# Another order of score stretches, sums and products in two hand-written turns of a two-layer attention and mixer kernel

## The chip, the cores and the metric

The kernel runs on one core of one Trainium2 chip. The metric is the device time of one execution in microseconds (us). Before the change the median of three runs was 2517.36 us, with the lowest at 2516.68 and the highest at 2517.88.

## The reference, cut to what matters

Two layers, each an attention (32 heads of 16 columns, one common key and value) and a token mixer, over 2048 tokens of 512 columns in float32:

```python
def _A_ref(x, wq, wk, wv, wo):          # B, S, D = 1, 2048, 512; H = 32, Dh = 16
    q = (x @ wq).reshape(B, S, H, Dh).transpose(0, 2, 1, 3)
    k, v = x @ wk, x @ wv
    scores = jnp.einsum("bhqd,bkd->bhqk", q, k) * (Dh ** -0.5)
    o = jnp.einsum("bhqk,bkd->bhqd", _softmax(scores, axis=-1), v)
    return o.transpose(0, 2, 1, 3).reshape(B, S, H * Dh) @ wo

def _B_ref(x, w1, b1, w2, b2):          # F = 1792
    u = _gelu(jnp.einsum("bsd,sf->bdf", _layernorm(x), w1) + b1)
    return (jnp.einsum("bdf,fs->bds", u, w2) + b2).transpose(0, 2, 1)

x = x + _A_ref(_layernorm(x), ...); x = x + _B_ref(_layernorm(x), ...)   # twice
```

## The kernel before, in words

**Stretches and groups.** The attention of a layer is cut into 1,024 stretches. A stretch holds the scores of two heads for 128 keys and 512 queries, which is a tile of 128x1024. There are 32 groups (four blocks of 512 queries, eight groups of four heads in each) of 32 stretches (16 key tiles, two pairs of heads). A stretch goes through three engines:

- `scores` (L903): TensorE (PE) makes the scores in a PSUM tile `sc` (matmuls at L909). There are three such tiles (`bank2`, two banks each), so a stretch can only be begun when the stretch three before it has been read out.
- ScalarE (ACT) takes the exponential out of `sc` into a tile `p` in SBUF (L919). In a "copied" stretch VectorE (DVE) first copies `sc` to `p` (L917) and ACT then works in place in `p`; the PSUM tile is free once the copy is done.
- `sums` (L921): PE multiplies `p` by the values into the accumulator `acc` of the group (L925). Two stretches of one key tile lie on different columns of the array. Stretches that are scored and not yet summed stand in `pend`; there are 8 tiles `p`, and 4 more from stretch 256 on.

**Products.** Between the stretches PE does matrix products of six matmuls of 128x128x512 each: the projections of finished heads with `wo` (tile `po`, L886, added to `x` by DVE at L894) and products of the mixer's first layer (tile `pu`, L1202; two of them make one result, which DVE copies or adds into `ua` at L1208 or L1210). DVE also does the normalization of rows of `x` that are finished (statistics at L1115 and L1116, the root at L218 to L233 and L203, the rows `hb` at L239, L1127 and L1131), the division of finished heads (L845 to L851) and the splitting of mixer weights (L1187, L1189). These small jobs wait in the list `steps`; `Mixer.step` takes jobs from it up to a budget.

**Turns.** The order of all this is written out by hand in tuples, called turns. `Attention.run` picks one when the last is done and goes through it: a number k above zero scores k stretches (13 is three, of which the last is copied; 12 is two, of which the last is copied); 0 is a product; -k sums the k oldest stretches of `pend` and then lets DVE do some of `steps`. The instructions of each engine stand in the order in which the turn names them, and each engine goes through its own in that order. In the queue of SyncE (SP) stand the loads of queries (`load_group`, issued when the second stretch of a group has been scored), of weights `w1r` and the moves of finished groups.

**Which turn is taken.** `to_boundary` is the number of stretches that must be summed until the group is finished. `PLAIN` (2, -2) is the turn when there is nothing to mix in. Up to stretch 270 two stretches stand in `pend` between turns (`LAG`); later four (once `normed` is above zero, the first block of rows being partly normalized). At stretch 270 of a layer, with 268 summed (`to_boundary` 20), the four projections of the first block's last heads are ready, and `Mixer.turn` returns `QUAD_TO_FOUR` with four projections: 32 stretches are scored and 30 summed, which takes `pend` from two to four. Four `PLAIN` turns follow, in which the last normalization of the block is done. At stretch 310, with 306 summed (`to_boundary` 14), the first two mixer products come, in the turn `COPIED`, 16 stretches long; a `DOUBLE` (32 stretches and four mixer products) is next. In the trace each of these two places comes once per layer: `QUAD_TO_FOUR` at 314.32 us and 1561.69 us, the first `pu` at 355.18 us and 1602.54 us.

Of the kernel before, what the change touches and what calls it, by code (L numbers as in the profile page):

```python
# [32 lines left out]
KEPT = 6  # L33
# [4 lines left out]
WHOLE = (13, 0, 0, 13, -4, 13, -4, 13, -4)  # L38
LONG = (2, 0, 13, -4, 13, -4, 13, 0, 13, -4, 12, -4)
COPIED = (13, 0, 12, 0, 13, -4, 13, -4, 3, -4, 2, -4)  # L40
DOUBLE = (
    13, -4, 13, 0, 0, 13, -4, 13, -4, 13, -4, 13, 0, 13, -4, 13, -4, 12, 0, 13, -4, 13, -4,
)
QUAD = (13, -4, 13, 0, 3, -6, 13, 0, 13, -4, 3, -4, 12, 0, 13, 0, 13, -6, 13, -4, 13, -4)
QUAD_TO_FOUR = (3, -2) + QUAD[2:]
FOURS = (3, -4, 12, 0, 13, 0, -4, 3, -4, 12, 0, 13, -4, 0)
SHORT = (2, 0, 3, -4, 3, -4)
TINY = (2, 0, 2, -4)
PLAIN = (2, -2)
# [20 lines left out]
def kernel(  # L70
# [18 lines left out]
    def pool(name, bufs=1, side="left"):  # L89
        return tc.alloc_tile_pool(name=name, bufs=bufs, side=side, reuse_waits="tile")  # L90
# [9 lines left out]
    def bank(i, name):  # L100
        return ps.tile([P, QB], F32, tag=f"ac{i % 2}", name=name)
# [146 lines left out]
    class Proj:  # L248
# [113 lines left out]
        def turn(self, ts_):  # L362

            self.transposes(ts_)
            self.first_rows(ts_)
            self.second_rows(ts_)
# [279 lines left out]
        def later(self, att):  # L646
# [3 lines left out]
            def put(turn, parts):  # L650
                work.append((turn, parts, None))
# [139 lines left out]
    class Attention:  # L791
# [185 lines left out]
        def size(self, turn):  # L977
            return sum(k % 10 for k in turn if k > 0)
# [6 lines left out]
        def run(self, mix, proj):  # L985


            total = 2 * NKT * NG * NB
            guards = [2 * NKT * g for g in sorted({2 * FIRST[self.l], NG})] + [total]
            self.guards = guards  # L990
            later, guarded, flagged = proj.later(self), 0, 0

            rest = range(NB - 2 if self.l == 0 else NB - 1, NB)
            turn, queued = FIRST_TURN[self.l], False
            parts = [lambda i, b=b: proj.values(b, i) for b in rest]
            while self.scored < total:
                mix.chores(self)
                ahead = min(t for t in guards if t > self.scored)
                known = ahead < guards[-2] or not later
                if ahead < total and self.scored >= ahead - 16 and flagged < ahead and known:  # L1000
                    flagged = ahead
                    proj.flag(proj.flagged)
                if turn is None:
                    turn = PLAIN
                    self.lag = 2 * LAG if mix.normed and self.scored < total - 16 else LAG
                    if len(self.pend) == self.lag:
                        after, queued = None, bool(later) and not mix.projections
                        if queued:
                            turn, parts, after = later[0]
                            if turn is WHOLE and self.to_boundary() >= 14 and self.slack(later) >= 4:  # L1010
                                turn = LONG
                        else:
                            turn, parts = mix.turn(self)
                            if turn is COPIED and not self.spares:
                                turn = LONG
                    left = min(t - self.scored for t in guards if t > self.scored)
                    if queued and turn is LONG and left < self.size(LONG):
                        turn = WHOLE
                    if left < self.size(turn):
                        turn = PLAIN  # L1020
                        if parts and mix.projections and left >= sum(k for k in SHORT if k > 0):
                            turn, parts = SHORT, parts[:1]
                    if turn in (LONG, COPIED) and self.to_boundary() in (2, 4, 2 * NKT):
                        turn = PLAIN
                    if turn is WHOLE and self.to_boundary() == 2:
                        turn = PLAIN
                parts = list(parts)
                for k in turn:
                    if k > 0:
                        self.more(mix, k)  # L1030
                    elif k == 0:
                        if queued and turn is TINY:
                            mix.step(2.0, self)
                        parts.pop(0)(self.spare())
                        if turn is DOUBLE and len(parts) % 2:
                            mix.step(1.0, self)
                        if queued and not parts:
                            later.pop(0)
                            if after:
                                after()  # L1040
                            if not later:
                                proj.close()
                                mix.open()
                    else:
                        if turn is PLAIN:
                            k = -min(4, max(0, len(self.pend) - self.lag))
                        end = self.to_boundary() <= -k
                        busy = self.behind
                        if busy:
                            self.behind = None  # L1050
                            busy()
                        self.drain(-k)
                        mix.chores(self)
                        if busy and turn is not DOUBLE:
                            continue
                        if self.pieces:
                            self.pieces.pop(0)()
                        elif turn in (LONG, COPIED, DOUBLE, QUAD, QUAD_TO_FOUR, FOURS, WHOLE):
                            room = 2.4 if turn in (COPIED, QUAD, QUAD_TO_FOUR) else 1.0
                            mix.step(min(room, 0.8 * self.to_boundary()), self)  # L1060
                        elif end:
                            mix.step(2.0, self)
                assert self.scored < guards[-2] or not later
                if self.scored in guards[:-1] and self.scored > guarded:
                    guarded = self.scored
                    i = guards.index(guarded)
                    proj.guard(guarded // (2 * NKT), guards[i + 1] // (2 * NKT))
                    if mix.opened:
                        self.spares = pool(f"more{self.l}")
                if turn is PLAIN and self.to_boundary() > 4:  # L1070
                    mix.step(1.7 if mix.normed else 2.4, self)
                turn = None


    class Mixer:
# [150 lines left out]
        def turn(self, att):  # L1226

            def projection(i):
                self.projection(att, i)

            def first(i):
                self.pu = bank(i, f"pu{self.l}_{self.done}")
                self.product(self.pu, stop=False)
                self.following()

            def second(_):
                r, f = self.product(self.pu, start=False)
                self.add(self.pu, r - 1, f)
                att.behind = self.following

            early = att.spares and att.scored < 2 * NKT * (NB * NG - 2) + 8
            if early and len(self.projections) > 3 and len(att.pend) == LAG and att.to_boundary() == 20:
                return QUAD_TO_FOUR, [projection] * 4
            early = early and att.to_boundary() in (26, 28, 30)
            if early and len(self.projections) > 3:
                return QUAD, [projection] * 4
            if len(self.projections) > 3 and att.to_boundary() == 30 and att.scored > 2 * NKT * (NB * NG - 1):
                return FOURS, [projection] * 4
            if len(self.projections) > 1:
                return COPIED, [projection] * 2  # L1250
            if self.projections:
                return SHORT, [projection]
            if early and (self.ready(KEPT + 1, 2) or self.last_pair_behind()):
                return DOUBLE, [first, second] * 2
            even = not att.spares or att.to_boundary() in (14, 30)
            return (COPIED, [first, second]) if even and self.ready(KEPT) else (PLAIN, [])

        def projection(self, att, which):

# [205 lines left out]
        def after(self, s):  # L1465
            self.split2(2 * s + 4)
# [115 lines left out]
    for layer in range(2):  # L1582
# [63 lines left out]
        if more:  # L1646
# [17 lines left out]
            second = proj.queries(b - 1, 1)  # L1664
# [59 lines left out]
```

## Time and profile before

| | |
|---|---|
| median of three runs | 2517.36 us |
| the profiled execution | 2514.03 us |
| its span, first to last instruction | 2512.3 us |
| PE busy | 2492.7 us (99%) |
| ACT busy | 2102.8 us (84%) |
| DVE busy | 1550.9 us (62%) |
| exponentials out of PSUM (L919, `p<-sc`) | 1444 of 1048 ns |
| exponentials of copied stretches (L919, `p<-p`) | 604 of 1084 ns |
| copies (L917) | 604 of 1224 ns |
| granted TensorE clock, mean | 0.999 |

How to read it: the span is one execution as the hardware profiler saw it, and the 1.73 us between it and the execution's own time lie before its first and after its last instruction. A busy PE is not a PE at its peak: its matmuls are pipelined, their ends are modelled, and a matmul that waits inside a run can be counted as busy. What a run of matmuls costs is therefore read below from the start of one run to the start of the next. In the timeline a line is start, duration, engine, source line, operation, tiles, shapes and the number of instructions merged; a bracket at its end tells how long the engine stood idle before it and who ended that. PE's count per stretch is two matmuls for scores and four for sums.

### The profile page before, as it was taken

The numbers are of one execution on the slowest core, as the hardware profiler recorded it, in microseconds if no ns is written. First come the engines' busy times: TensorE is split into PE (matmuls) and PEld (weight loads), VectorE is DVE, ScalarE is ACT, GpSimd is POOL, SyncE is SP. The second block draws the span as 40 slices with busy tenths as digits, with TensorE's granted clock in tenths as the row PEclk, the third lists the DMA queues.
The fourth block names the chain that finished last, engine by engine and source line by source line (L and its number), as shares of the span: only waits on it lengthen the run. The fifth ranks groups of instructions, "written<-read, shape, count | busy, mean of one in ns | idle before, by whom it ended". The sixth has DMA issues, their size and how long they took to land. (4 is left out here: it accounts for less than half of the span.)

```text
span 2512.3 us, 41954 instructions
## 1 busy us (share of the span) xinstructions
PE 2492.7 (99%) x16158; PEld 1240.3 (49%) x16158; DVE 1550.9 (62%) x2458; ACT 2102.8 (84%) x2344; POOL 147.8 (6%) x235
## 2 busy tenths in 40 slices
PE   9999999999999999999999999999999999999999
PEld 6444334444444444588863443344444444445887
DVE  6565566667766776564445664666677667765522
ACT  6999999999999999653349999999999999995511
POOL 5000000000000000141000000000000000002200
PEclk9999999999999999999999999999999999999999
DMA  3221201111111111134423211111111111102343
GB/s 116 75 66 41 65 27 41 31 42 31 39 31 39 31 41 31 43 110 149 128 58 118 61 45 48 31 39 31 41 31 39 31 42 33 40 26 66 107 125 95
DMA packets 168679, 143.56 MB, mean 57 GB/s; under 512 B 17650, under 2 KB 132368, under 8 KB 167952
## 3 DMA queue, kind: packets, MB, share of 16 engines
q1 hardware_dynamic: 168464, 140.72, 19.3%
q8 instruction: 132, 2.16, 0.4%
q14 instruction: 83, 0.68, 0.1%
HBM read 97.67 MB, written 26.22 MB: 49 GB/s over the span
## 5 line engine op out<-in xcount | busy, mean ns | idle before, releaser
L919 ACT ACTIVATE p<-sc 128x1024 f32<-128x1024 f32 x1444 | 1404.4, 1048 | 62.6 <-PE sc L909 61.9
L917 DVE COPY p<-sc 128x1024 f32<-128x1024 f32 x604 | 739.1, 1224 | 520.8 <-PE sc L909 436.8
L925 PE MATMUL acc<-p,vaug 128*32 128x512 f32 x8192 | 999.3, 599 | 0.5 <-DVE q L528 0.5
L909 PE MATMUL sc<-qs,kst 51*128 51x512 f32 x4096 | 684.9, 432 | 10.2 <-ACT p L919 3.3
L919 ACT ACTIVATE p<-p 128x1024 f32<-128x1024 f32 x604 | 654.8, 1084 | 16.4 <-DVE p L917 11.0
L909 PEld LDWEIGHTS sc<-qs,kst 51*128 51x128 f32 x4096 | 338.1, 184 | 564.3 <-ACT p L919 393.8
L925 PEld LDWEIGHTS acc<-p,vaug 128*32 128x32 f32 x8192 | 218.8, 109 | 488.7 <-issue 472.5
L1455 PE MATMUL py<-u,w 128*128 128x512 f32 x1344 | 307.4, 390 | 0.0
L1455 PEld LDWEIGHTS py<-u,w 128*128 128x128 f32 x1344 | 251.9, 188 | 52.3
L1443 ACT CAST w<-w2r 128x896 fp32r<-128x896 f32 x64 | 60.3, 945 | 184.9 <-PE py L1455 177.3
L1202 PE MATMUL pu<-hb,w 128*128 128x512 f32 x792 | 209.6, 406 | 0.0
L1202 PEld LDWEIGHTS pu<-hb,w 128*128 128x128 f32 x792 | 140.9, 188 | 57.6 <-issue 31.1
L1189 POOL TENSOR_TENSOR w<-w1r,w 128x256 fp32r<-128x256 f32 x86 | 69.7, 818 | 1586.1 <-ACT w L1187 1584.0
L1444 DVE TENSOR_TENSOR w<-w2r,w 128x896 fp32r<-128x896 f32 x64 | 71.9, 1123 | 111.5 <-ACT w L1443 111.2
L845 DVE RECIPROCAL o<-o 128x128 f32<-128x128 f32 x120 | 113.3, 944 | 8.7 <-DMA o<-ev 8.7
L886 PE MATMUL po<-wo,hl 128*128 128x512 f32 x360 | 100.3, 412 | 0.1
L827 DVE COPY ev<-acc 128x512 f32<-128x512 f32 x64 | 43.7, 683 | 69.1 <-PE acc L925 69.1
L415 PE MATMUL pq<-hT,wq 128*128 128x512 f32 x312 | 81.1, 404 | 0.0
L886 PEld LDWEIGHTS po<-wo,hl 128*128 128x128 f32 x360 | 62.6, 188 | 33.6 <-issue 15.9
L1202 PE MATMUL pu_l<-hb,w 128*128 128x512 f32 x336 | 77.1, 389 | 0.0
L1461 DVE SCALAR_TENSOR_TENSOR x<-py,b2c,x 128x512 f32<-128x512 f32 x32 | 24.0, 750 | 81.2 <-PE py L1455 81.2
L1187 ACT CAST w<-w1r 128x256 fp32r<-128x256 f32 x86 | 34.4, 406 | 47.2 <-PE pu_l L1202 12.8
(191 smaller groups left out, 1179.3 us busy)
## 6 DMA issues: line engine op xcount, KB each, us to landing
w1r<-in_B_w_dram SPq DMA_DIRECT2D x224, 128.0 KB
w2r<-in_B_w_dram SPq DMA_DIRECT2D x64, 448.0 KB
qs<-qd SPq DMA_DIRECT2D x384, 64.0 KB
qd<-q SPq DMA_DIRECT2D x64, 256.0 KB
o<-ev SPq DMA_DIRECT2D x128, 128.0 KB
x<-in_A_x_dram SPq DMA_DIRECT2D x16, 256.0 KB
hd<-hT SPq DMA_DIRECT2D x2, 2048.0 KB
out_dram<-x SPq DMA_DIRECT2D x16, 256.0 KB
```

The lines of the kernel that those rows point to most:

```text
L415: yield nc.tensor.matmul(out, a, c, start=(k == 0), stop=(k == len(terms) - 1))
L845: nc.vector.reciprocal(o[:, 1, c], o[:, 1, c])
L886: nc.tensor.matmul(po, a, c, start=(k == 0), stop=(k == 3 * len(parts) - 1))
L909: nc.tensor.matmul(sc[:, j, :], kst[kt // 4][rows, kt % 4 * P : (kt % 4 + 1) * P], qs[i % NQ][rows, j0 // 2, :], start=True, stop=True,)
L917: nc.vector.tensor_copy(pt, sc)
L919: nc.scalar.activation(pt, sc, AF.Exp, scale=0.25)
L925: nc.tensor.matmul(self.acc[i][c : c + 32, :], vaug[:, kt].rearrange("p d k -> p (d k)"), pt[:, j, :], start=(kt == 0), stop=(kt == NKT - ...
L1189: eng.tensor_tensor(w[:, 1], raw, f32(w[:, 0]), op=ALU.subtract)
L1202: nc.tensor.matmul(pu, a, c, start=(start and k == 0), stop=(stop and k == 5))
L1443: nc.scalar.copy(w[:, 0], raw)
L1444: nc.vector.tensor_tensor(w[:, 1], raw, f32(w[:, 0]), op=ALU.subtract)
L1455: nc.tensor.matmul(py, a, d, start=(c == 0 and f == 0 and k == 0), stop=(c == 1 and f == NFH - 1 and k == 2),)
```

## The change

Two tuples and the places that name them. `QUAD_TO_FOUR` had been `QUAD` with another first pair of entries; it is now written out in an order of its own. `ENTRY` is new and takes the place of `COPIED` where `Mixer.turn` returns a pair of mixer products; projections that use `COPIED` keep it. `ENTRY` is given the same budget for `steps` as `COPIED`.

```diff
 QUAD = (13, -4, 13, 0, 3, -6, 13, 0, 13, -4, 3, -4, 12, 0, 13, 0, 13, -6, 13, -4, 13, -4)
-QUAD_TO_FOUR = (3, -2) + QUAD[2:]
+QUAD_TO_FOUR = (
+    2, -2, 13, 0, 13, -4, 13, 0, 13, -4, 3, -6, 13, 0, 13, 0, 3, -6, 13, -4, 3, -4,
+)
+ENTRY = (1, 0, 13, 0, 13, -4, 13, -4, 13, -4, 13, -4)
...
-                        elif turn in (LONG, COPIED, DOUBLE, QUAD, QUAD_TO_FOUR, FOURS, WHOLE):
-                            room = 2.4 if turn in (COPIED, QUAD, QUAD_TO_FOUR) else 1.0
+                        elif turn in (LONG, COPIED, ENTRY, DOUBLE, QUAD, QUAD_TO_FOUR, FOURS, WHOLE):
+                            room = 2.4 if turn in (COPIED, ENTRY, QUAD, QUAD_TO_FOUR) else 1.0
...
-            return (COPIED, [first, second]) if even and self.ready(KEPT) else (PLAIN, [])
+            return (ENTRY, [first, second]) if even and self.ready(KEPT) else (PLAIN, [])
```

Written one above the other, before and after:

```
stretch 270, before: 3 -2 13 0  3 -6 13 0 13 -4 3 -4 12 0 13 0 13 -6 13 -4 13 -4
stretch 270, after:  2 -2 13 0 13 -4 13 0 13 -4 3 -6 13 0 13 0  3 -6 13 -4  3 -4
stretch 310, before: 13 0 12 0 13 -4 13 -4  3 -4  2 -4
stretch 310, after:   1 0 13 0 13 -4 13 -4 13 -4 13 -4
```

## The prediction

> **What bounds the kernel now.** The page comes first: the span and the share of PE.
>
> ```profile
> span 2512.3 us, 41954 instructions
> ...
> PE 2492.7 (99%) x16158; PEld 1240.3 (49%) x16158; DVE 1550.9 (62%) x2458; ACT 2102.8 (84%) x2344; POOL 147.8 (6%) x235
> ...
> L1202 PE MATMUL pu<-hb,w 128*128 128x512 f32 x792 | 209.6, 406 | 0.0
> ```
>
> PE is counted busy for 99% of the span, but a matmul that waits inside a run is counted too, so the page cannot show whether the two turns lose anything. The table by stretches of time puts a number on it: the two changed turns and the four `PLAIN` turns between them, in layer 0, then a `DOUBLE` cycle for comparison, then the same three in layer 1.
>
> ```profile
> 314.32:345.45 31.13, 30.59 (x211) 12.65 (x210) 20.81 (x42) 29.74 (x32) 0.00 (x0) 1.00 0.07 22
> 345.45:353.42 7.97, 7.23 (x52) 2.11 (x48) 6.88 (x22) 7.27 (x9) 0.00 (x0) 1.00 0.01 3
> 353.42:369.80 16.38, 15.96 (x113) 6.38 (x109) 7.53 (x10) 16.00 (x18) 0.00 (x0) 1.00 0.15 42
> 741.73:772.30 30.57, 30.57 (x218) 12.92 (x216) 24.17 (x38) 29.62 (x33) 0.00 (x0) 1.00 0.14 40
> 1561.69:1592.81 31.12, 30.59 (x212) 12.64 (x210) 20.94 (x42) 29.75 (x32) 0.00 (x0) 1.00 0.08 22
> 1592.81:1600.79 7.98, 7.24 (x53) 2.11 (x49) 6.88 (x22) 7.28 (x9) 0.00 (x0) 1.00 0.01 2
> 1600.79:1617.13 16.34, 15.93 (x112) 6.39 (x108) 7.53 (x10) 15.98 (x18) 0.00 (x0) 1.00 0.15 42
> ```
>
> The first number after the window is its length. The changed region takes 31.13 + 7.97 + 16.38 = 55.48 us in layer 0 and 31.12 + 7.98 + 16.34 = 55.44 in layer 1, so one walk serves both. The clock is 1.00 in all of them. What it would take without a wait comes from PE's timeline, read from the start of one run to the start of the next.
>
> ```profile
> 312.49 0.73 PE L909 MATMUL sc<-qs,kst 51*128 51x512 f32 x4
> 313.15 1.24 PE L925 MATMUL acc<-p,vaug 128*32 128x512 f32 x8
> 314.32 1.35 PE L909 MATMUL sc<-qs,kst 51*128 51x512 f32 x6
> 315.60 1.07 PE L925 MATMUL acc<-p,vaug 128*32 128x512 f32 x8
> 316.60 0.91 PE L909 MATMUL sc<-qs,kst 51*128 51x512 f32 x4
> 317.92 0.49 PE L909 MATMUL sc<-qs,kst 51*128 51x512 f32 x2 [0.42 <-ACT p L919]
> 318.34 1.67 PE L886 MATMUL po<-wo,hl 128*128 128x512 f32 x6
> 319.94 0.97 PE L909 MATMUL sc<-qs,kst 51*128 51x512 f32 x6
> 320.84 2.78 PE L925 MATMUL acc<-p,vaug 128*32 128x512 f32 x24
> 323.55 0.97 PE L909 MATMUL sc<-qs,kst 51*128 51x512 f32 x6
> 324.45 1.65 PE L886 MATMUL po<-wo,hl 128*128 128x512 f32 x6
> 326.03 0.96 PE L909 MATMUL sc<-qs,kst 51*128 51x512 f32 x6
> 326.93 1.92 PE L925 MATMUL acc<-p,vaug 128*32 128x512 f32 x16
> 328.78 0.96 PE L909 MATMUL sc<-qs,kst 51*128 51x512 f32 x6
> ...
> 345.45 0.73 PE L909 MATMUL sc<-qs,kst 51*128 51x512 f32 x4
> 346.11 1.06 PE L925 MATMUL acc<-p,vaug 128*32 128x512 f32 x8
> 347.11 0.49 PE L909 MATMUL sc<-qs,kst 51*128 51x512 f32 x2
> 348.34 0.49 PE L909 MATMUL sc<-qs,kst 51*128 51x512 f32 x2 [0.74 <-ACT p L919]
> 348.77 1.06 PE L925 MATMUL acc<-p,vaug 128*32 128x512 f32 x8
> ...
> 353.42 0.90 PE L909 MATMUL sc<-qs,kst 51*128 51x512 f32 x4
> 354.75 0.50 PE L909 MATMUL sc<-qs,kst 51*128 51x512 f32 x2 [0.42 <-ACT p L919]
> 355.18 1.67 PE L1202 MATMUL pu<-hb,w 128*128 128x512 f32 x6
> ```
>
> Without a wait, three score stretches take 326.93 - 326.03 = 0.90, two 346.11 - 345.45 = 0.66, one 348.77 - 348.34 = 0.43; two sums 347.11 - 346.11 = 1.00, four 328.78 - 326.93 = 1.85, six 323.55 - 320.84 = 2.71; a product 326.03 - 324.45 = 1.58. As a test, `DOUBLE` is ten runs of three, one of two, eight of four sums and four products: 9.00 + 0.66 + 14.80 + 6.32 = 30.78, and its window took 30.57, so it waits for nothing. `QUAD_TO_FOUR` is ten runs of three, one of two, two, four times four and twice six sums, four products: 9.00 + 0.66 + 1.00 + 7.40 + 5.42 + 6.32 = 29.80. Four `PLAIN` are 4 x 1.66 = 6.64. `COPIED` is 3.60 + 1.32 + 7.40 + 3.16 = 15.48. Together that is 51.92 against 55.48: **3.56 us of waiting per layer**, 1.33 in `QUAD_TO_FOUR`, 1.33 in the `PLAIN` turns, 0.90 in `COPIED`.
>
> Where they lie can be read in the same rows. The run of three at 314.32 takes 1.28 and the next one, at 316.60, takes 1.74 until the product at 318.34: 0.38 and 0.84 too long. The `PLAIN` at 347.11 needs 1.66 for its two scores instead of 0.66, and `COPIED`, at 353.42, 1.76 for three instead of 0.90. All of them wait for a PSUM tile that ACT, or the copy on DVE, has not yet emptied. ACT and DVE at these places:
>
> ```profile
> 302.18 17.52 ACT L919 ACTIVATE p<-sc 128x1024 f32<-128x1024 f32 x19 [0.83 <-PE sc L909]
> 319.77 1.06 ACT L919 ACTIVATE p<-p 128x1024 f32<-128x1024 f32 x1
> 320.73 2.83 ACT L919 ACTIVATE p<-sc 128x1024 f32<-128x1024 f32 x3
> ...
> 346.32 1.06 ACT L919 ACTIVATE p<-p 128x1024 f32<-128x1024 f32 x1 [0.70 <-DVE p L917]
> 347.28 9.24 ACT L919 ACTIVATE p<-sc 128x1024 f32<-128x1024 f32 x10
> ...
> 370.40 1.94 ACT L919 ACTIVATE p<-sc 128x1024 f32<-128x1024 f32 x2 [0.35 <-PE sc L909]
> ```
>
> ```profile
> 344.26 0.69 DVE L1115 BATCH_NORM_STATS2 stb<-x 128x6 f32<-128x512 f32 x1
> ...
> 345.08 1.20 DVE L917 COPY p<-sc 128x1024 f32<-128x1024 f32 x1
> ```
>
> ACT runs without a gap from 302.18 through 19 exponentials, 17.52 / 19 = 0.92 each, and a copied one costs 320.73 - 319.77 = 0.96. A `PLAIN` gives ACT 1.84 of work in 1.66 of PE's, so PE is held back to ACT's pace before stretch 270 (312.49 to 314.32 is 1.83) and comes to the turn with ACT a full set of tiles behind. The wait at 347.11 has another origin: DVE did row statistics (344.26) ahead of the copy at 345.08, ACT stood idle for 0.70 until that copy was done (346.32), and PE then found all three PSUM tiles still taken.
>
> **The change part by part.** The work is the same. `QUAD_TO_FOUR` keeps eleven score runs of the same sizes, seven sums and four products; `ENTRY` has 0.43 + 5 x 0.90 = 4.93 of scores where `COPIED` had 4.92. Copies go from eight to seven in the one and from four to five in the other, together none added. The slots in which DVE may take small jobs stay seven and four, with the same budgets, so the jobs keep their sequence. SP keeps its order too: the query load waits for the same stretch, used some 30 stretches later, and the `w1r` loads follow the same products. The largest number of stretches in `pend` is twelve in either order, as many as there are tiles `p`, and the sums that free the tile of the next exponential stand ahead of its scores in PE's queue, so that costs nothing. Only the waits can change.
>
> *The head of the turn at 270.* Call the stretch scored at 314.32 s1. The row of 19 gives the ends of the exponentials: s0 at 302.18 + 14 x 0.92 = 315.06, s1 315.98, s2 316.90, s3 317.82, s4 318.74. Two scores end at 314.98; the two sums then wait for s0 as in the `PLAIN` at 313.15, which took 1.17, until 316.15. Of the next three, s5 needs the tile of s2: 316.90, and 0.10 for the release (the run at 317.92 against s3's 317.82). It is issued at 317.00 and the product follows at 317.00 + 0.43 = 317.43, where it was 318.34: **0.91 earlier**. While PE does it, ACT clears more than a stretch.
>
> *The rest of that turn.* From 317.43 there are nine runs of three, four of four sums, two of six and four products: 8.10 + 7.40 + 5.42 + 6.32 = 27.24, to 344.67 if nothing waits. ACT goes on from s4: s5 is copied and its exponential starts 319.77 - 318.34 = 1.43 after the product, 318.86, ending 319.82; from there three stretches with one copied are 2 x 0.92 + 0.96 = 2.80: s8 322.62, s11 325.42, s14 328.22. The close places are s13, which PE reaches at 324.47 and which needs s10 at 322.62 + 2 x 0.92 + 0.10 = 324.56, and s16, reached at 327.22, which needs s13 at 327.36. That is 0.09 and 0.14; I take 0.2 for the middle and end the turn at **344.87**, 0.58 earlier than 345.45.
>
> *The `PLAIN` turns.* The new turn ends on three stretches that are not copied, so no copy stands behind the statistics. The last copied stretch is s29, scored by 340.27; its exponential ends 320.73 - 318.34 = 2.39 later, 342.66, and I add 0.3 because the group's end and normalization jobs stand ahead of its copy on DVE. Three more at 0.92 end at 345.72, 0.85 after the turn; before it was 346.32 + 0.96 = 347.28, 1.83 after. With half of ACT's debt gone the 1.00 at 347.11 goes. What is late next is ACT's own pace: 0.17 per `PLAIN` once the lead is used up, in two of the four by my count, so 0.3 in all. They end at 344.87 + 6.64 + 0.3 = **351.81**, where it was 353.42.
>
> *`ENTRY` at 310.* It asks for one tile ahead of the product: that of s38, whose exponential ends at 345.72 + 6 x 0.92 = 351.24, in time. After the product, at 353.82, s42 to s44 need s39 to s41, at 352.16, 353.08 and 354.00, all there. So it takes its 15.49 and ends at **367.30**, where it was 369.80. The rows for its two products must be normalized by then; DVE works them off in one piece after its copies and is moved earlier by the lost copy, so that cover stays. If it were not, each 1 us of lateness beyond the first product would cost 1 us.
>
> *What follows.* In `ENTRY` the first copied stretch is s44; its run ends at 354.72, its exponential 2.39 later at 357.11, and four runs at 2.80 end with s56 at 368.31, 1.0 after PE. Before, ACT was done at 370.40 - 0.35 = 370.05, 0.25 after PE. A `DOUBLE` leaves ACT 30.57 - 29.62 = 0.95 of idle while PE waits for nothing, so it takes up the 0.75 more.
>
> Sum: 369.80 - 367.30 = 2.50 per layer, 5.0 for two. Bounds: with none of the 0.2 and 0.3, 3.0 per layer; with 0.17 in all four `PLAIN` turns and ACT's 0.70 back behind the copy of s29, 2.5 - 0.4 - 0.7 = 1.4. The profiled execution would go from 2514.03 (span 2512.3) to 2509.0. It lies 3.3 under the median of the runs shown, 2517.36, which becomes **2512.3**.
>
> **The rivals.** First, *the waits move and stay*: there are three PSUM tiles before and after, ACT needs 1.84 per `PLAIN`, and whatever PE gains at the head it gives back at the next place where it is three stretches ahead. Then only the 0.91 at 318.34 lasts: 2517.36 - 1.82 = 2515.5. For it speaks the 1.83 of the `PLAIN` at 312.49; against it the `DOUBLE` that waits for nothing with the same three tiles, and ACT's 0.70, which is no lack of tiles. The Trainium skill, Perfetto Trace Analysis, section Optimization Strategy, has a rule that would favour this rival: the same gap coming again and again on the engine that should be full can mean too little PSUM for the next tile. By that rule the 0.17 agrees, the single gaps of 1.00 and 0.84 do not. Second, *all of it goes*: 3.0 per layer, 2511.3. Third, and slower, *the debt is carried on*: ACT enters the first `DOUBLE` 0.75 later against PE than now. From a debt of more than the 0.95 that a `DOUBLE` gives back it would stay, and PE would wait, say 0.42 (the row at 317.92), in each. 792 matmuls are 132 products, 66 per layer, two in `COPIED` and 64 in 16 `DOUBLE` turns: 16 x 0.42 - 2.50 = 4.2 per layer, 2525.8. Later `DOUBLE` turns without a wait speak against it. Fourth, *`ENTRY` is not taken*, because the normalization isn't finished at 310; then the head's gain alone remains, 2515.5.
>
> **How the numbers follow.** Forecast 0.57, with a range of its own from 2511.6 to 2513.6; waits that stay 0.22, all goes 0.13, debt 0.06, not taken 0.02. A measurement of this kernel can tell about 0.2% from no change, 5.0 us: the border, 2512.3, runs through the forecast. Half of it (0.29) and the second rival (0.13) give faster 0.42; the other half (0.28), the first and the fourth give the same, 0.52; the debt gives slower, 0.06. The range goes from 2510.6, below the second rival by the spread of the runs, to 2515.4, which leaves out part of the first rival, the fourth and the debt.
>
> **What would show it.** In the changed profile: the first `po` of the turn 3.1 us after its start (4.0 now); the four `PLAIN` turns in about 6.9 (7.97 now) with no wait of 0.7; the first `pu` after one score stretch and without an idle ahead of it; the region in 53.0 in either layer; `DOUBLE` still 30.6. Wrong would be a wait ahead of the run of three that follows the second product, an ACT idle above 0.5 for a copy, `DOUBLE` cycles of 31, or a change of the time that lies outside the two regions.

## The result, and the profile after

The changed kernel took 2511.65 us, the median of 17 runs (2510.29 to 2515.04). The kernel before, run beside it, took 2517.36 us (17 runs, 2514.59 to 2518.29). The ratio is 0.9979, with a 95% interval of 0.9973 to 0.9986. Forecast were 2512.3 us, in a range of 2510.6 to 2515.4. The profiled execution took 2510.91 us, where before it was 2514.03.

On the page after, the span has changed and the share of PE has not:

```profile
span 2509.2 us, 41946 instructions
...
PE 2492.8 (99%) x16158; PEld 1240.5 (49%) x16158; DVE 1550.9 (62%) x2458; ACT 2101.7 (84%) x2344; POOL 148.2 (6%) x235
```

The table by stretches of time has the same seven windows as before: the turn at 270, the four `PLAIN` turns and the turn at 310 in layer 0, a `DOUBLE` cycle, and the three of layer 1. The first number behind a window is its length; then come the busy times of PE, PE's weight loads, DVE, ACT and POOL, the clock and the DMAs.

```profile
315.81:346.48 30.67, 30.55 (x211) 12.68 (x210) 21.14 (x42) 29.64 (x32) 0.00 (x0) 1.00 0.07 22
346.48:353.62 7.14, 7.14 (x52) 2.11 (x48) 6.37 (x23) 7.14 (x9) 0.00 (x0) 1.00 0.02 3
353.62:369.12 15.50, 15.50 (x112) 6.51 (x109) 7.88 (x9) 15.06 (x18) 0.00 (x0) 1.00 0.15 44
742.91:773.48 30.57, 30.57 (x218) 12.91 (x217) 24.16 (x39) 29.62 (x33) 0.00 (x0) 1.00 0.14 40
1560.80:1591.47 30.67, 30.55 (x211) 12.69 (x209) 21.34 (x42) 29.63 (x32) 0.00 (x0) 1.00 0.07 22
1591.47:1598.61 7.14, 7.14 (x52) 2.12 (x49) 6.37 (x23) 7.14 (x9) 0.00 (x0) 1.00 0.01 2
1598.61:1614.10 15.49, 15.49 (x114) 6.50 (x110) 7.89 (x9) 15.06 (x18) 0.00 (x0) 1.00 0.15 44
```

| us, layer 0 | turn 270 | four `PLAIN` | turn 310 | region |
|---|---|---|---|---|
| before | 31.13 | 7.97 | 16.38 | 55.48 |
| forecast | 30.55 | 6.94 | 15.49 | 52.98 |
| after | 30.67 | 7.14 | 15.50 | 53.31 |

All three parts became shorter, by 0.46, 0.83 and 0.88, which makes 2.17 in layer 0; layer 1 gained 55.44 - 53.30 = 2.14. Together that is 4.31 us. The lowest times of the two kernels differ by 2514.59 - 2510.29 = 4.30, and the `DOUBLE` cycle is the same to 0.01. That the 4.30 meets the 4.31 so closely is chance: for `entry_only` below, the lowest times differ by 2514.46 - 2510.50 = 3.96, where its regions gain 1.7. The two profiled executions differ by 3.12 only, because what lies ahead of the first region took 1.49 more in the second of them (315.81 against 314.32). That part is the same code in all kernels of this study, and in their profiles it ended anywhere from 314.2 to 318.1 us (the paragraph on the median shows what goes with it). So below it is the regions that are compared, and not spans.

Where the time went is in PE's timeline after (a line is start, duration, engine, source line, operation, tiles and the number of matmuls; the code stands three lines lower than before, so L912 is scores, L928 sums, L889 and L1205 products):

```profile
315.81 0.73 PE L912 MATMUL sc<-qs,kst 51*128 51x512 f32 x4
316.47 1.24 PE L928 MATMUL acc<-p,vaug 128*32 128x512 f32 x8
317.64 1.35 PE L912 MATMUL sc<-qs,kst 51*128 51x512 f32 x6
318.92 1.66 PE L889 MATMUL po<-wo,hl 128*128 128x512 f32 x6
...
325.75 1.05 PE L912 MATMUL sc<-qs,kst 51*128 51x512 f32 x6
326.73 1.92 PE L928 MATMUL acc<-p,vaug 128*32 128x512 f32 x16
328.59 0.99 PE L912 MATMUL sc<-qs,kst 51*128 51x512 f32 x6
329.51 2.78 PE L928 MATMUL acc<-p,vaug 128*32 128x512 f32 x24
...
337.16 1.18 PE L912 MATMUL sc<-qs,kst 51*128 51x512 f32 x6
338.27 2.78 PE L928 MATMUL acc<-p,vaug 128*32 128x512 f32 x24
...
346.48 0.74 PE L912 MATMUL sc<-qs,kst 51*128 51x512 f32 x4
347.14 1.07 PE L928 MATMUL acc<-p,vaug 128*32 128x512 f32 x8
348.14 0.89 PE L912 MATMUL sc<-qs,kst 51*128 51x512 f32 x4
348.96 1.06 PE L928 MATMUL acc<-p,vaug 128*32 128x512 f32 x8
349.96 0.90 PE L912 MATMUL sc<-qs,kst 51*128 51x512 f32 x4
...
351.78 0.91 PE L912 MATMUL sc<-qs,kst 51*128 51x512 f32 x4
352.63 1.07 PE L928 MATMUL acc<-p,vaug 128*32 128x512 f32 x8
353.62 0.49 PE L912 MATMUL sc<-qs,kst 51*128 51x512 f32 x2
354.05 1.67 PE L1205 MATMUL pu<-hb,w 128*128 128x512 f32 x6
```

The first product starts 318.92 - 315.81 = 3.11 after the turn, as forecast; it was 4.02. The wait of 0.7 in the second `PLAIN` is gone, and the first `pu` follows one score stretch at once. But the runs of three at 325.75, 328.59 and 337.16 take 0.98, 0.92 and 1.11 until the next run, together 0.31 over the 0.90 that each needs. And three of the four `PLAIN` turns take 1.82, 1.82 and 1.84, which is ACT's pace, where the forecast had two at most.

### The profile page after: what moved, and what is told of

The parts are those of the page before. It is cut to its first block, busy times and chain, and to the rows that moved or that the text cites. A ratio compares the mean times of both kernels' runs of the same rounds, so it can differ in the third digit from the quotient of the medians.

```text
span 2509.2 us, 41946 instructions
## 1 busy us (share of the span) xinstructions
PE 2492.8 (99%) x16158; PEld 1240.5 (49%) x16158; DVE 1550.9 (62%) x2458; ACT 2101.7 (84%) x2344; POOL 148.2 (6%) x235
## 5 line engine op out<-in xcount | busy, mean ns | idle before, releaser
L928 PE MATMUL acc<-p,vaug 128*32 128x512 f32 x8192 | 1000.1, 599 | 0.5 <-DVE q L531 0.5
L912 PE MATMUL sc<-qs,kst 51*128 51x512 f32 x4096 | 683.5, 432 | 6.8 <-SPq L630 2.7
L912 PEld LDWEIGHTS sc<-qs,kst 51*128 51x128 f32 x4096 | 338.3, 184 | 559.5 <-ACT p L922 387.3
L928 PEld LDWEIGHTS acc<-p,vaug 128*32 128x32 f32 x8192 | 219.0, 109 | 489.3 <-issue 472.9
L1205 PE MATMUL pu<-hb,w 128*128 128x512 f32 x792 | 209.6, 406 | 0.0
L1205 PEld LDWEIGHTS pu<-hb,w 128*128 128x128 f32 x792 | 140.9, 188 | 57.7 <-issue 31.9
L889 PE MATMUL po<-wo,hl 128*128 128x512 f32 x360 | 100.4, 412 | 0.1
L889 PEld LDWEIGHTS po<-wo,hl 128*128 128x128 f32 x360 | 62.6, 188 | 33.9 <-issue 16.0
L1205 PE MATMUL pu_l<-hb,w 128*128 128x512 f32 x336 | 77.1, 389 | 0.0
```

The lines of the kernel that those rows point to most:

```text
L889: nc.tensor.matmul(po, a, c, start=(k == 0), stop=(k == 3 * len(parts) - 1))
L912: nc.tensor.matmul(sc[:, j, :], kst[kt // 4][rows, kt % 4 * P : (kt % 4 + 1) * P], qs[i % NQ][rows, j0 // 2, :], start=True, stop=True,)
L928: nc.tensor.matmul(self.acc[i][c : c + 32, :], vaug[:, kt].rearrange("p d k -> p (d k)"), pt[:, j, :], start=(kt == 0), stop=(kt == NKT - ...
L1205: nc.tensor.matmul(pu, a, c, start=(start and k == 0), stop=(stop and k == 5))
```

## The experiments

My theory after the result was that the three gains have three causes that add up: the order in the turn at 270, the last run of that turn that isn't copied, and the one stretch ahead of the product at 310. The rival was that they hang together, ACT's debt being carried from one to the next, so that one part alone gains little or all. Four kernels take the change apart. `turn270_only` is the changed kernel with `COPIED` again at 310, `entry_only` is the kernel before with `ENTRY`, and two more exchange the end of the turn:

```diff
 e3: before, the last run not copied
-QUAD_TO_FOUR = (3, -2) + QUAD[2:]
+QUAD_TO_FOUR = (3, -2) + QUAD[2:-2] + (3, -4)
 e4: after, the last run copied
-    2, -2, 13, 0, 13, -4, 13, 0, 13, -4, 3, -6, 13, 0, 13, 0, 3, -6, 13, -4, 3, -4,
+    2, -2, 13, 0, 13, -4, 13, 0, 13, -4, 3, -6, 13, 0, 13, 0, 3, -6, 13, -4, 13, -4,
 e1: after, COPIED at 310; e2: before, ENTRY at 310 (with its budget)
-            return (ENTRY, [first, second]) if even and self.ready(KEPT) else (PLAIN, [])
+            return (COPIED, [first, second]) if even and self.ready(KEPT) else (PLAIN, [])
```

> The new order at stretch 270, the old turn COPIED at 310. Theory (each wait goes where its cause goes): turn 270 as in the changed kernel, 30.7 us per layer (31.13 before), PLAIN turns 7.1 (7.97 before), COPIED keeps its wait for the third score tile, 16.35; region 54.2 per layer, so 1.3 less than 55.48 and about 2.6 us less for the kernel. Rival (the waits move and stay): the gain at the head is given back at the next place, region 55.0 or more, COPIED longer than 16.4.

> The old order at 270, the new turn at 310. Theory: turn 270 and the PLAIN turns as before, 31.13 and 7.97, the turn at 310 in 15.5 (16.38 before); region 54.6, 0.9 less per layer, about 1.8 us for the kernel. The two parts together give what the change gave (2.2 per layer). Rival (waits move): with ACT as far behind as before, the runs of three after the first product wait instead, turn at 310 16.2 or more, or the DOUBLE cycle behind it is longer than 30.6.

> The kernel before with one entry changed: the last run of three of the turn at 270 is not copied (3 instead of 13). Theory (the wait of 1.00 in the PLAIN turns comes from the copy that stands behind row statistics on DVE): ACT's idle of 0.70 is gone, the wait in the PLAIN turns falls from 1.00 to about 0.3, PLAIN turns 7.2 (7.97 before), the turn at 270 unchanged at 31.1, COPIED unchanged at 16.4: region 54.7. Rival (too few tiles, ACT's pace): PLAIN turns stay above 7.7 since ACT has as many exponentials to do as before.

> The changed kernel with one entry changed: the last run of three of the turn at 270 is copied (13 instead of 3). Theory: the copy stands behind normalization and row statistics on DVE, ACT waits 0.6 to 0.9 for it, and the PLAIN turns take 7.6 to 7.9 instead of 7.14; the turn at 270 and the one at 310 stay at 30.7 and 15.5. Rival (the head alone pays): PLAIN turns stay at 7.1.

| us, layer 0 | turn 270 | four `PLAIN` | turn 310 | region |
|---|---|---|---|---|
| before | 31.13 | 7.97 | 16.38 | 55.48 |
| e3: before, last run not copied | 31.11 | 7.14 | 16.35 | 54.60 |
| e2: before, `ENTRY` | 31.13 | 7.97 | 15.50 | 54.60 |
| e4: after, last run copied | 30.67 | 7.98 | 15.50 | 54.15 |
| e1: after, `COPIED` at 310 | 30.67 | 7.15 | 16.34 | 54.15 |
| after | 30.67 | 7.14 | 15.50 | 53.31 |

(Read from the start of the turn's first scores to the start of the runs that follow the 32nd, 40th and 56th stretch on PE's timeline; layer 1 agrees within 0.04.) The parts add up: the order gives 31.13 - 30.67 = 0.46, the last run 7.97 - 7.14 = 0.83, `ENTRY` 16.38 - 15.50 = 0.88, each of the same size whether the others are there or not. The rival is out. `turn270_only` and `entry_only` were also run often enough for a median: 2511.48 for the one (11 runs; before beside it 2516.22; ratio 0.9981, 0.9972 to 0.999) and 2512.9 for the other (11 runs; 0.999, 0.9981 to 0.9999). The regions say 2.6 and 1.7 us for the two. The medians say 4.7 and 3.3; that agrees within their intervals, which could not have split it, but both lie above.

**Is it the copy, or what stands ahead of it?** In the kernel before, the last copy of the turn stood on DVE behind row statistics, and ACT was idle for 0.70. One kernel leaves the order of before and lets DVE take its small jobs a little later:

```diff
-                            room = 2.4 if turn in (COPIED, QUAD, QUAD_TO_FOUR) else 1.0
+                            room = 2.38 if turn is QUAD_TO_FOUR else 2.4 if turn in (COPIED, QUAD) else 1.0
```

> The kernel before with its old orders; only the budget for small jobs in the turn at 270 goes from 2.4 to 2.38, so that the first row statistics of the second pair (0.8) no longer fit ahead of the last copied run and come one slot later. Theory (lateness of the copy, not the copy itself): with the last run still copied, the PLAIN turns fall from 7.97 to 7.1 to 7.3 as they did when that run was not copied (7.14); ACT's idle of 0.70 goes; turn at 270 31.1, at 310 16.4, region 54.6 to 54.8. Rival (a copied last run costs it, since it lengthens the way to the exponential): PLAIN turns stay at 7.7 to 8.0.

On DVE's timeline of that kernel the copy now stands first, and it starts 0.96 earlier than before (344.12 against 345.08, in executions whose turns begin within 0.11 of each other):

```profile
344.12 1.22 DVE L917 COPY p<-sc 128x1024 f32<-128x1024 f32 x1
345.25 0.68 DVE L1115 BATCH_NORM_STATS2 stb<-x 128x6 f32<-128x512 f32 x1
```

The region took 54.62, with `PLAIN` turns of 7.16: the whole 0.83 without any change of the turn. So it was the place in DVE's queue, and not the copy. A budget smaller by 0.02 did as much as that part of the change.

**`ENTRY`: one stretch, or the copies?** One kernel has two stretches ahead of the product in layer 0, and in layer 1 `COPIED` with its first run not copied:

```diff
+ENTRIES = (2, 0, 12, 0, 13, -4, 13, -4, 13, -4, 13, -4), (3,) + COPIED[1:]
...
-            return (ENTRY, [first, second]) if even and self.ready(KEPT) else (PLAIN, [])
+            return (ENTRIES[self.l], [first, second]) if even and self.ready(KEPT) else (PLAIN, [])
```

> The changed kernel with another turn at 310 in each layer. Layer 0: 2 0 12 0 13 -4 13 -4 13 -4 13 -4, two stretches ahead of the first product. Layer 1: COPIED with its first run not copied, 3 0 12 0 13 -4 13 -4 3 -4 2 -4. Theory (each stretch asked for ahead of the product waits for ACT's pace): layer 0 15.65 to 15.75 (15.50 with one), layer 1 16.35 as COPIED has it. Rival (it is the copy in the first run that costs): layer 1 15.5.

The turn at 310 took 15.68 and 16.36. Two stretches ahead cost one wait of 0.18, three cost 0.87 (16.36 against 15.49), as with `COPIED`, and copying the first run has no part in it. That is the prediction's reason as it stood.

**Why not all of the head's gain stayed.** The product came 0.91 earlier and the turn ended 0.46 earlier. If PE's waits were what costs, a product still earlier or shorter should bring more. `product_first` takes it ahead of the first sums; `short_product` leaves out the second half of one projection (three of its six matmuls; the first product in layer 0, the third in layer 1):

```diff
 e6
-    2, -2, 13, 0, 13, -4, 13, 0, 13, -4, 3, -6, 13, 0, 13, 0, 3, -6, 13, -4, 3, -4,
+    2, 0, 13, -2, 13, -4, 13, 0, 13, -4, 3, -6, 13, 0, 13, 0, 3, -6, 13, -4, 3, -4,
 e10
-            att.project(parts, t, bank2(name)[:, 0, :] if which is None else bank(which, name))
+            short = parts[-1] == 3 and t == (0, 2)[n]
+            att.project(
+                parts[:1] if short else parts, t, bank2(name)[:, 0, :] if which is None else bank(which, name)
+            )
```

> The changed kernel with the first product one place earlier: 2 0 13 -2 instead of 2 -2 13 0. Theory: two scores fit into free tiles, the product follows 0.66 after the start, and the run of three after it finds its tiles empty, so the 0.54 of the head go; ACT's pace gives some of it back in the middle. Turn at 270 30.2 to 30.5 (30.67 in the changed kernel), PLAIN turns 7.1 to 7.4, region 53.0 (53.31). Rival (the waits move): all of it comes back, region 53.3.

> The changed kernel with one projection of the turn at 270 cut to three of its six matmuls (it leaves out the second half of the heads' product there): in layer 0 the first product, at the head, in layer 1 the third, behind the first six sums. That is 0.68 less work for PE. Theory (ACT sets the pace from the head on, and only ACT's idle can be won): layer 0, turn at 270 and PLAIN turns together 0 to 0.2 shorter than 37.81; layer 1 0.3 to 0.5 shorter, as much as ACT's idle behind the sums allows. Rival (PE's work and waits add up): both 0.6 to 0.7 shorter.

`product_first`: turn 30.81, region 53.47, so 0.14 and 0.16 longer than in the changed kernel, where 0.2 to 0.5 less had been expected for the turn. Its product came 2.4 us earlier still, and the waits were back at the next place, as its rival had it. From the timeline of PE, and then of ACT:

```profile
322.96 0.73 PE L912 MATMUL sc<-qs,kst 51*128 51x512 f32 x4 [0.21 <-ACT p L922]
```

```profile
320.96 1.94 ACT L922 ACTIVATE p<-sc 128x1024 f32<-128x1024 f32 x2 [0.23 <-PE sc L912]
```

`short_product`: 53.35 and 53.33 against 53.31 and 53.30, though PE has 0.69 less to do: in layer 1 the short product takes 1581.33 - 1580.44 = 0.89 until the next run instead of 1.58. PE stands idle in the scores behind it, which it did not in the changed kernel:

```profile
1580.44 0.96 PE L889 MATMUL po<-wo,hl 128*128 128x512 f32 x3
1581.33 0.50 PE L912 MATMUL sc<-qs,kst 51*128 51x512 f32 x2
1582.16 0.73 PE L912 MATMUL sc<-qs,kst 51*128 51x512 f32 x4 [0.33 <-ACT p L922]
```

I had expected 0.3 to 0.5 there. Less work on the engine that is busy 99% of the span gained nothing at all, so from the start of this turn to the end of the `PLAIN` turns PE does not set the pace. That ACT does is inferred from the sum of its work, and from e3 and e5, where 0.75 and 0.77 less idle on ACT gained 0.85 and 0.84; no kernel took work off ACT alone. It has 40 exponentials of 0.92 there, and 0.04 more for each copied one (rows of the prediction): 36.80 + 7 x 0.04 = 37.08. PE without a wait has 29.80 + 6.64 = 36.44. By this sum only ACT's idle time can count. After, it is three gaps, 0.37 + 0.34 + 0.24 = 0.95:

```profile
332.84 1.94 ACT L922 ACTIVATE p<-sc 128x1024 f32<-128x1024 f32 x2 [0.37 <-PE sc L912]
...
341.58 1.94 ACT L922 ACTIVATE p<-sc 128x1024 f32<-128x1024 f32 x2 [0.34 <-PE sc L912]
343.76 1.06 ACT L922 ACTIVATE p<-p 128x1024 f32<-128x1024 f32 x1 [0.24 <-DVE p L920]
344.73 11.08 ACT L922 ACTIVATE p<-sc 128x1024 f32<-128x1024 f32 x12
```

Before, with the 0.70 at 346.32, it was five, 2.03 together:

```profile
324.15 1.94 ACT L919 ACTIVATE p<-sc 128x1024 f32<-128x1024 f32 x2 [0.59 <-PE sc L909]
...
333.64 1.06 ACT L919 ACTIVATE p<-p 128x1024 f32<-128x1024 f32 x1 [0.18 <-DVE p L917]
...
340.56 1.94 ACT L919 ACTIVATE p<-sc 128x1024 f32<-128x1024 f32 x2 [0.32 <-PE sc L909]
342.74 1.06 ACT L919 ACTIVATE p<-p 128x1024 f32<-128x1024 f32 x1 [0.24 <-DVE p L917]
```

**Three kernels with other idle times** put this count to the test, and try for a better version. Each has its own turn at 270 in either layer:

```diff
+QUADS = (   # e9
+    (2, -2, 13, 0, 13, -4, 13, 0, 13, -4, 3, -6, 13, 0, 13, 0, 3, -6, 3, -4, 3, -4),
+    (2, -2, 3, 0, 3, -4, 3, 0, 3, -4, 3, -6, 3, 0, 3, 0, 3, -6, 3, -4, 3, -4),
+QUADS = (   # e11
+    (2, -2, 13, 0, 13, -4, 13, 0, 13, -4, 3, -6, 13, 0, 13, 0, 3, -4, 13, -4, 3, -4),
+    (2, -2, 13, 0, 13, -4, 13, 0, 13, -4, 3, -4, 13, 0, 13, -2, 0, 3, -4, 13, -4, 3, -4),
+QUADS = (   # e12
+    (2, -2, 13, 0, 13, -4, 13, 0, 13, -4, 3, -6, 13, 0, 13, 0, 3, -4, 3, -4, 3, -4),
+    (2, -2, 13, 0, 13, -4, 13, 0, 13, -4, 3, -6, 13, 0, 13, 0, 13, -4, 3, -4, 3, -4),
...
-                return QUAD_TO_FOUR, [projection] * 4
+                return QUADS[self.l], [projection] * 4
```

> The changed kernel with fewer copied runs in the turn at 270. Layer 0: the last copied run (13 ahead of the last but one sum) is not copied, so no exponential of the end stands behind normalization on DVE. Layer 1: no run of that turn is copied. Theory (from the head of the turn to the last PLAIN it is ACT's idle that counts): layer 0 loses ACT's idle of 0.24 and the PLAIN turns fall from 7.14 to 6.9 to 7.0, turn at 270 30.7, region 53.1; layer 1, tiles come free only with the exponential, PE waits more in the runs of three but ACT has 7 x 0.04 less to do: turn at 270 30.7 to 31.2, PLAIN turns 7.1 or less. Rival (PE's own waits add up, copies are what keeps tiles free): layer 0 53.3 or more, layer 1 turn at 270 above 31.5.

> The changed kernel, with other sums in the turn at 270, a different variant in each layer. Layer 0: the second six sums become four, so that two more stretches stay unsummed at the end of the turn and the first PLAIN sums four. Layer 1: that, and the first six sums are cut into four, three scores, two and a product. ACT idles after each six sums (0.34 to 0.37) because three tiles hold 2.75 of work for it while PE sums for 2.71 and then scores. Theory (only ACT's idle counts from the start of the turn to the end of the PLAIN turns, and it comes from the long sums): turn and PLAIN turns together take 37.81 minus what idle goes, 37.4 to 37.6 in layer 0 and 37.1 to 37.4 in layer 1, and the turn at 310 stays 15.5. Rival: the idle comes back elsewhere or PE's waits take its place, 37.75 to 37.85 in both. Second rival: small DVE jobs stand ahead of a copy again, over 38.2 in one of them.

> The changed kernel, with a turn at 270 in which the second six sums are four (two more stretches stay unsummed at its end) and no copied stretch follows the sums that end the group. Layer 0: the last copied stretch of the turn is not copied at all. Layer 1: the copied stretch is put one run earlier, ahead of the sums that end the group, so that its copy stands ahead of the eviction and the normalization on DVE. Theory (only ACT's idle counts): the 0.34 after the second six sums goes and the 0.24 to 0.70 for a late copy does not come, so turn and PLAIN turns together take 37.3 to 37.55 in each layer (37.81 in the changed kernel, 38.18 where the late copy stood behind the normalization). Rival: with fewer copies or an earlier one, PE waits for tiles instead and nothing is gained, 37.7 to 37.9. The turn at 310 stays 15.5. The whole kernel is 0.6 to 1.0 below the changed one, less than runs of this kernel differ.

The next table has the time from the start of the turn at 270 to the end of the `PLAIN` turns on PE, the idle times of ACT in it, and what is left when the idle and 36.80 + 0.04 per copied exponential are taken off.

| us | time | ACT idle | copied | left |
|---|---|---|---|---|
| before | 39.10 | 0.59 + 0.18 + 0.32 + 0.24 + 0.70 = 2.03 | 8 | -0.05 |
| e3, last run not copied | 38.25 | 0.55 + 0.18 + 0.31 + 0.24 = 1.28 | 7 | -0.11 |
| e5, statistics later | 38.26 | 0.55 + 0.16 + 0.31 + 0.24 = 1.26 | 8 | -0.12 |
| e4, last run copied | 38.65 | 0.37 + 0.34 + 0.24 + 0.70 = 1.65 | 8 | -0.12 |
| after | 37.81 | 0.37 + 0.34 + 0.24 = 0.95 | 7 | -0.22 |
| e6, product first | 37.96 | 0.23 + 0.37 + 0.34 + 0.25 = 1.19 | 7 | -0.31 |
| e10, short product, layer 1 | 37.81 | 0.36 + 0.34 + 0.24 = 0.94 | 7 | -0.21 |
| e9, one copy less, layer 0 | 37.75 | 0.36 + 0.35 + 0.18 = 0.89 | 6 | -0.18 |
| e9, no copies, layer 1 | 39.10 | 0.17 + 0.19 + 0.77 + 1.01 + 0.18 = 2.32 | 0 | -0.02 |
| e11, two left unsummed, layer 0 | 38.18 | 0.36 + 0.70 + 0.21 = 1.27 | 7 | -0.17 |
| e11, and six sums split, layer 1 | 39.62 | 0.40 + 1.90 + 0.21 = 2.51 | 7 | 0.03 |
| e12, no late copy, layer 0 | 38.01 | 0.36 + 0.20 + 0.58 = 1.14 | 6 | -0.17 |

Over a spread of 1.9 us the count holds within 0.33, and what is left is negative where PE ends a little further ahead of ACT than it began. Work and idle time of any engine add up to about the length of a stage, so the table by itself shows no cause. It shows that the few idle times listed are all there is, and which of them come and go. As versions they disappoint. e9 without copies is 1.3 longer: its rival was right, the copies are what keeps the PSUM tiles free for PE, and ACT idles 0.77 and 1.01 after the six sums. With one copy less, in layer 0, the region was expected at 53.1 and took 53.26: the idle of 0.24 went, but one of 0.18 came in the `PLAIN` turns. e11, in layer 0, takes away the gap of 0.34 after the second six sums and gets 0.70 for it, since the group's end now comes directly ahead of the last copied run (in the changed kernel two more sums lie between), and the copy has the whole of the normalization before it. From DVE's timeline, and ACT's:

```profile
343.75 0.69 DVE L1138 TENSOR_TENSOR hb<-ht,hb 128x512 fp32r<-128x512 f32 x1
344.36 1.22 DVE L924 COPY p<-sc 128x1024 f32<-128x1024 f32 x1
```

```profile
345.61 1.06 ACT L926 ACTIVATE p<-p 128x1024 f32<-128x1024 f32 x1 [0.70 <-DVE p L924]
```

In layer 1 splitting the first six sums did not take their gap away (0.40), and the last copy had row statistics before it too: ACT idled 1.90 for it. So e11's second rival, small jobs ahead of a copy, came true.

e12 mends that, and was expected at 37.3 to 37.55; it took 38.01 and 38.06, above its rival's 37.9 too. The two sums that were put off now stand in `PLAIN` turns, where PE sums four (1.85) and ACT has only two stretches (1.84) until the next scores. On ACT's timeline the gap has only moved:

```profile
346.34 4.69 ACT L926 ACTIVATE p<-sc 128x1024 f32<-128x1024 f32 x5 [0.20 <-PE sc L916]
351.60 6.52 ACT L926 ACTIVATE p<-sc 128x1024 f32<-128x1024 f32 x7 [0.58 <-PE sc L916]
```

e11 had a median of 2513.2 (11 runs; ratio 0.999, 0.9981 to 0.9999) and e12 of 2511.08 (11 runs; 0.9977, 0.9968 to 0.9987). The latter doesn't differ from the changed kernel by more than runs do, and its regions are 0.2 and 0.3 longer. Of all twelve only layer 0 of e9 is below the changed kernel in its region, by 0.05.

**Was there cover for ACT's debt?** The prediction let a `DOUBLE` absorb what `ENTRY` leaves on ACT, 0.95 being idle. One kernel gives ACT exponentials of a single number behind `ENTRY`, three in layer 0 and ten in layer 1:

```diff
+                if turn is ENTRY:
+                    for _ in range((3, 10)[self.l]):
+                        warm(AF.Exp)
```

> The changed kernel with extra work on ACT behind the turn at 310: 3 one-element exponentials in layer 0, 10 in layer 1, at 0.2 us each. Theory (a DOUBLE gives back what ACT owes): layer 0, 0.6 more, the DOUBLE cycle behind it takes 30.6 to 30.8; layer 1, 2.0 more, it takes 31.4 to 32.1 and the DOUBLE after that 30.6 again. Rival (debt is carried on): both layers' second DOUBLE longer than 30.8 too.

The ten took 1615.39 - 1614.46 = 0.93, not the 2.0 that I had priced them at, and the three some 0.28. The `DOUBLE` behind them took 30.77 and 31.43 instead of 30.58 and 30.57, and the one after that 30.57 and 30.60. From ACT's and from PE's timeline in layer 1:

```profile
1614.46 1.02 ACT L196 ACTIVATE warm<-onerow 1x1 f32<-1x1 f32 x10
1615.39 1.90 ACT L922 ACTIVATE p<-sc 128x1024 f32<-128x1024 f32 x2
...
1621.53 1.94 ACT L922 ACTIVATE p<-sc 128x1024 f32<-128x1024 f32 x2 [0.54 <-PE sc L912]
```

```profile
1617.34 0.73 PE L912 MATMUL sc<-qs,kst 51*128 51x512 f32 x4 [0.40 <-ACT p L922]
```

PE lost 0.19 of 0.28, and 0.86 of 0.93, at the next scores; there is room for less than 0.1 at that place. The idle time of the `DOUBLE` lies behind it (0.54 at 1621.53), after two products, and it keeps the loss from being carried on. So the expectation of an absorbed 0.6 was wrong, though both cycles lie in the ranges expected, 30.6 to 30.8 and 31.4 to 32.1: the load was half of what I had reckoned, and most of it was lost. The rival's loss in every later cycle did not come either.

## Why the prediction was right, and where it was not

**The head, right.** The tile of the stretch three before set the second run, to the digit: 3.11 forecast and measured.

**The rest of the turn, mis-sized by 0.12.** The term "I take 0.2 for the middle" was 0.31, and most of it lay elsewhere. The run with s13, at 325.75, lost 0.08 (0.09 forecast) and the run with s16, at 328.59, 0.02 (0.14 forecast). The other 0.21 is at 337.16, the run that stands ahead of the second six sums, for which the forecast had no term. The turn took 30.67, not 30.55.

**The `PLAIN` turns, right in the cause, mis-sized by 0.20.** No copy stands behind the statistics, and the 1.00 is gone (e3 and e5 show that this is the cause). But "0.17 per `PLAIN` in two of the four" was three of four and 0.50 in all.

**The step behind both that failed** is that the forecast walked along PE and added up PE's waits. From 344.87 - 314.32 + 6.94 = 37.49 it is short of the 37.81 by 0.32, nearly all of the 0.33 that the region misses. ACT's 37.08 of work and its idle were not summed. With them the forecast could have seen that six sums of 2.71 leave ACT three stretches, some 2.8, until the next scores are made, so that it idles there in every order run here that keeps them: in the changed kernel 0.37 and 0.34 for the two, and 0.24 for the copy behind the normalization that was known (the 0.3 "because the group's end and normalization jobs stand ahead"). That sum, 37.08 + 0.95 = 38.03, is itself 0.22 too long; it names the places better than it gives the length.

**`ENTRY`, right**: 15.50 against 15.49, no wait ahead of the product, for the reason given (e7). ACT ends it 370.04 - 369.12 = 0.92 behind PE, with 1.0 forecast.

**What follows, right in the number and wrong in its reason.** The next `DOUBLE` took 30.58. But its 0.95 of idle is no cover at the place where it would be needed (e8): there is room for 0.1. It went well because 0.92 behind is just what the `DOUBLE` bears at its start. A debt above that would have cost its own size once per layer, not the 0.42 in 16 turns of the third rival.

**The median, right by two errors that cancel.** The regions gave 4.3 where the forecast had 5.0; with that alone the median would be 2517.36 - 4.3 = 2513.1. Measured is 2511.65, 1.4 lower. The forecast went to 2509.0 for the profiled execution and added the 3.3 by which the median of before lies over its profile. The profile took 2510.91, 1.9 more than forecast, and the median lies only 0.74 over it. So the 2511.65 bears out the way and the rough size, and that it lies so near 2512.3 is luck.

The traces show where executions differ outside the regions. In windows of 20 us up to 2500, the granted clock of every profile rounds to 1.00 in all but two places, 40 to 60 and 1280 to 1320 us, ahead of the first region and between the two. There it differs from one execution to the next, and the length of those parts goes with it:

| granted clock, 45 to 60 us | profiles | start of the first region, us |
|---|---|---|
| 1.00 | before, e5, e7, e9 | 314.2 to 314.9 |
| 0.89 | after, e4, e8 | 315.3 to 316.3 |
| 0.77 | e1, e2, e3, e6, e10, e11, e12 | 316.4 to 318.1 |

| granted clock, 1290 to 1310 us | profiles | from the first region's end to the second's start, us |
|---|---|---|
| 1.00 | e1, e2, e3, e8 | 1190.3 to 1190.6 |
| 0.91 | before, after, e5, e7, e9, e10, e11 | 1191.6 to 1192.2 |
| 0.83 | e4, e6, e12 | 1193.2 to 1193.5 |

As an estimate, 15 us at 0.77 instead of 1.00 hold back 15 x 0.23 = 3.4 us of matmul time, which fits the size. The profile of before had the first place at 1.00, and so it lies low among its runs. Whether such differences also make the 1.4 stays open, because for the other runs only the mean clock of the whole execution is on record. The gap isn't particular to this change: the medians of all five kernels with 11 or 17 runs gained more than their regions, by 0.7 to 2.3 us, and that all five lie on one side is unexplained.

**The first rival**, waits that move and stay, is half seen: of the head's 0.91, 0.46 stays. The Trainium skill, Perfetto Trace Analysis, section Optimization Strategy, says that a gap which keeps coming back on the engine that should be full can mean too few buffers. The 0.16 to 0.18 of three `PLAIN` turns is such a gap by its look, and here it is the difference of two engines' work (1.84 for two exponentials, 1.66 for PE), so by that sum more tiles would not take it away; it wasn't tried. The same page's section Identifying the Most-Contended Engine warns that the busy share of matmuls is no good measure of how close TensorE is to its limit, while occupancy is a fair one for ScalarE. This case fits that: in the turn at 270 and the `PLAIN` turns PE is counted busy for 37.69 of 37.81 and ACT for 36.78, and yet 0.69 less work on PE gained nothing.

## What to carry to other kernels

Where two engines take turns on a stage, add up the work of each for that stage, idle times and all, before adding up the waits of one of them: in this case the idle of the engine with more work was the only time to be had, and 0.69 less work on the other gained nothing. A copy that feeds the pacing engine belongs ahead of small jobs in its own engine's queue; look at what stands before it there, since 0.02 in a job's budget can be worth as much as a new order. And idle time covers a delay only if it comes before the next place where the other engine needs the result.

## What was not expected of the hardware

Ten exponentials of one number each took 0.93 us from the start of the first to the start of the next instruction, 0.093 each, where I had reckoned with 0.2. An exponential of 128x1024 takes 0.92 from the start of one to the next out of PSUM (12 in 11.08) and about 0.96 in place in SBUF.
